# Banded attention and a gated FFN on one core: values matmuls joined to later scores, and other buffers for sums of weights

## The chip, the cores and the metric

One core of a Trainium2 chip runs the whole kernel. The metric is the device time of one execution in microseconds, the median of several runs; the parts of a profile come from one further execution. TensorE, VectorE (DVE), ScalarE (ACT), GpSimd (POOL) and SP's DMA queue each work through a list of their own in order, and wait for one another through semaphores.

## The reference

Eight batches of 576 positions with eight heads of 64 channels go through attention in a band: a query sees itself and the 63 positions before it. The result, as 4608 tokens of 512 channels, goes through a feed-forward network of 2048 hidden units with a gate in place of an activation. All is float32.

```python
scores = (q @ k.T) / sqrt(64)                    # per batch and head
mask = (rel >= 0) & (rel < 64)                   # rel: query position - key position
attn = softmax(where(mask, scores, -1e9))
x = (attn @ v)  as 4608 x 512
h = x @ w_in                                     # 512 x 2048
g = where(h >= 1, h, where(h <= -1, 0, (h + 1) ** 2 / 4))
out = g @ w_out                                  # 2048 x 512
```

## The kernel before, in words

**Tiles and steps.** The tokens are cut into nine tiles of 512. Attention makes a tile in four *steps* of 128 tokens (two blocks of 64 queries, all eight heads). A step has, on TensorE, its **scores** (`att_scores`, L408, small matmuls into two banks `ps_a`) and its **values** (`att_values`, L483, small matmuls from the transposed probabilities `ptd` and the loaded `vt`). Between them lie a mask (L425), a maximum (L429), exponentials on ScalarE (L436), a normalization (L448) and twelve transposes on VectorE (L454). Behind the values, `x_take` copies the bank out to a buffer `u` (L264 on ScalarE, L266 on VectorE), and after two of a tile's steps `add_build` forms the operands of the FFN from it: four differences (L537), then high and low parts (L264/L266 and L549), on ScalarE, VectorE or GpSimd.

**The FFN in three-part products.** Every float32 operand is split into a high and a low part, and a product is the sum of three matmuls. Tiles 0 and 1 multiply x by the weights as they are (`ffn_in`, L877). Tiles 2 to 8 take a pair of hidden chunks at a time, in eight pairs (`ffn_products`, L828): seven products in place of eight, from sums of weights and of x, put together by additions on VectorE (`h_add`, L844). 12 + 12 products come first, then 6 + 12, all into the two banks `ps_h`. The gate follows (ScalarE L889 and L894, VectorE L901, casts L906, low parts on GpSimd L911), and then the output products (L928) into four banks `acc`; gh and gl in the rows below are the gate's high and low part.

**Sums of weights.** They are made once, during tile 1, for the eight pairs (`add_sums`: L736, L745, a cast on ScalarE, L755), and written to DRAM (`kept`). From tile 2 on, each pair's seven operands are loaded from there into *rings* (`add_ring`, `ring_load`) shortly before their use.

**Buffers.** The first layer's weights take 16 places in SBUF, which come free after tile 1 (and after the sums that read them). The tables `X_PIECES`, `R_PIECES`, `H_SLOT` and `TMP_SLOT` say who gets which: operands of x for even and for odd tiles, rings, the hidden values h, and the scratch in which sums are made. In the kernel before, the scratch of pairs 2 to 7 is place 3 and, for the second half of pairs 3 to 7, place 0, which is also that of h: so the first products of tile 2 wait for the sums of the last pair to be kept.

**Order.** A planner (`Plan`) lays all work out before the kernel is built. Each piece of work has a key (about when it is due), costs on the engines that may do it, what it waits for, and slots that it takes from pools and gives back (`ps_a`, `ps_h`, `acc`, `u`, ...). It fills each engine's list with what can start first, lower keys ahead. A whole tile is 21.3 units of keys long. `S_LATE`, `S_LATER` and `S_PACE` set the keys of sums, `A_EARLY` how early the steps of tiles 3 to 8 are due.

**Joined steps.** In `add_step`, a step that is `joined` hands its values on: they are done in one piece with the scores of the next step in the list, by one entry of the planner that also takes a `ps_h` bank for them. Before, steps of tile 2 but its last are joined. All others do their values alone, into a bank of `ps_a`, once the transposes are there. The steps of a tile come in the order 0, 2, 1, 3.

Of the kernel before, what the change touches and what calls it, by code (L numbers as in the profile page):

```python
# [10 lines left out]
F32 = mybir.dt.float32  # L11
# [9 lines left out]
P = 128  # L21
# [18 lines left out]
SOON = 8  # L40
# [46 lines left out]
S_LATE = 3  # L87
S_LATER = 3
S_PACE = 2
X_KEY = 1.3  # L90
# [4 lines left out]
EARLY_2 = 1.5  # L95
X_PIECES = (4, 5, 2), (14, 15)
R_PIECES = (6, 8), (10, 12)
H_SLOT = "w0_0", "w1_0"
TMP_SLOT = "w3_0"
R_LEAD = 6  # L100
R_LOAD = 2800, 2100
A_EARLY = 5

# [89 lines left out]
def banded_attention_then_ffn(ctx: ExitStack, tc: tile.TileContext, q, k, v, w, masks, out, dims):  # L193
# [316 lines left out]
    def x_tiles(t):  # L510
        if t in xops:
            return
        shape = [P, 2, 2, 2, 2 * SB]
        a, b = (xpool.tile(shape, F32R, name="xs", tag=f"{n}{t % 2}") for n in ("xh", "xl"))
        rest = [piece(f).rearrange("p (a c n) -> p a c n", a=2, c=2) for f in X_PIECES[t % 2]]
        if t % 2:
            rest.append(wpool.tile(shape[:1] + shape[2:], F32R, name="xs", tag=TMP_SLOT))
        xops[t] = a, b, rest, [rest[0], a[:, 1], b[:, 0], a[:, 0], rest[1], b[:, 1], rest[2]]
# [66 lines left out]
    def add_step(t, i):  # L585
# [3 lines left out]
        masked = s < PE_MASKS  # L589
        joined = SOON <= s and t <= PLAIN and i < TILES[t] // SB - 1  # L590
        pt, pv = ("ps_h", "acc") if s < LENT else ("ps_a", "ps_a")
# [135 lines left out]
    def sum_whole(n, c, i, eng):  # L727
        if i:
            pass
        elif n < 2:  # L730
            half_of[n, c] = [xpool.tile([P, 8, P], F32, name="half", tag=("xh0", "xl0")[c])]
        else:
            half_of[n, c] = [wpool.tile([P, 8, P], F32, name="half", tag=H_SLOT[0] if n > 2 and c else TMP_SLOT)]
        t = half_of[n, c][0]
        w_ = by_chunk(n)[i]
        engine[eng].tensor_tensor(  # L736
            out=t[:, 2 * i:2 * i + 2], in0=w_[:, 0, c].bitcast(F32), in1=w_[:, 1, c].bitcast(F32), op=ALU.add
        )
# [26 lines left out]
    def add_sums(n):  # L765
        key = step(1) + S_PACE * n + (S_LATE if n < 2 else S_LATER)
        ready = [w_ready[2 * n, 0], w_ready[2 * n + 1, 0]]
        xp = add(key, dict(SP=2000), lambda e: sum_pass(n), ready + [x_in[0]], lag=O_LAG_DMA)
        reads, keeps = [xp], [xp]
        for c in range(2):  # L770
            after = ready + ([x_in[0]] if n < 2 else [l1[1, 3], *sums_read[1]]) + sum_last
            if n == 2 and c:
                after.append(keeps[-1])
            elif n == 3 and not c:
                after.append(sums_kept[2][-1])
            elif n > 2 and c:
                after += [l1[1, 0], *sums_read[0]]
            k = key + c * S_PACE / 2
# [16 lines left out]
    def ring_load(t, n, i):  # L795
        rings[t, n, i] = r = []
        for part in range(2):
            m = 4 - i
            r.append(piece(R_PIECES[i][n % 2] + part)[:, :2 * m * P].rearrange("p (c o n) -> p c o n", c=2, o=m))
            nc.sync.dma_start(out=r[part].bitcast(F32), in_=kept[n][:, part, :, R_OPS[i]])  # L800
# [3 lines left out]
    def add_ring(t, n, i, key):  # L804
        after = [*sums_kept[n], *ring_last[i]]
        if t == PLAIN and n < 2:
            m = R_PIECES[i][n % 2] // 2
            after += [l1[1, 2 * m], l1[1, 2 * m + 1], *sums_read[m]]
        x = add(
# [36 lines left out]
    def add_products(t, n, key, after):  # L846
        ra, rb = (add_ring(t, n, i, key) for i in range(2))
        needs = [ra, *after]
        if t == PLAIN and n < 2:
            needs += [l1[1, 0], l1[1, 1], *sums_read[0], *sums_kept[NF // 2 - 1]]  # L850
        cost, take = dict(DVE=75 + 256 * 1.04), dict(ACT=80 + 256 * .83, DVE=75 + 256 * 1.05)
# [222 lines left out]
    for t in range(len(TILES)):  # L1074
# [4 lines left out]
        if t + 1 == PLAIN:  # L1079
            for n in range(NF // 2):  # L1080
                add_sums(n)
            x_after[t + 1] = [l1[1, f] for f in (2, 4, 5)] + sums_read[1] + sums_read[2] + sums_kept[0] + sums_kept[1]
            x_after[t + 2] = [l1[1, NF - 1], *sums_read[7], *sums_kept[7]]
# [58 lines left out]
```

## Time and profile before

| | |
|---|---|
| runs | 891.44, 891.52, 892.87 us; median 891.52 |
| profiled execution | 890.89 us, span 889.1 us |
| granted TensorE clock | 0.994 |
| TensorE busy | 869.5 us (98%) |
| VectorE, ScalarE, GpSimd busy | 650.4, 508.0, 268.8 us |
| stages of the span | up to some 120 us the first steps and tile 0; then tile 1 with the sums; tile 2 from about 240; from 330 on a tile takes some 94 us; the last tile from 796 has no attention beside it |

How to read the rows: a group's row gives line, engine, operation, output and inputs, shapes and count, then busy time and the mean of one in ns, then the idle time of the engine ahead of it. A row of the timeline gives start, length, engine, line, operation and count, in brackets the idle time ahead and what ended it. Matmuls overlap, so a row's length goes past the start of the next; starts are what counts. One matmul in the program of scores or values is two in the trace (32 become 64, 16 become 32). Windows give the busy time of each engine in a stretch. A wait names who waited, for whom, total us, times, longest.

### The profile page before, as it was taken

What the parts mean: (1) busy time and instruction counts of PE and PEld (TensorE: products, weight loads), DVE (VectorE), ACT (ScalarE), POOL (GpSimd) and SP (SyncE); (2) the same over time, 40 slices, a digit from 0 to 9 for tenths busy, and PEclk for the clock granted to TensorE, in tenths of its full rate; (3) what the DMA queues carried; (4) which work ended last, traced back from release to release, by engine and by line L of the source; (5) the groups of instructions that cost most, each with busy time, mean ns of one, the idle gap of its engine ahead of it and who ended that gap; (6) DMA issues with size and microseconds to landing.
All of it is one profiled execution on the core that took longest, in us unless ns stands there. A gap on an engine that the chain in (4) does not pass through costs nothing.

```text
span 889.1 us, 20426 instructions
## 1 busy us (share of the span) xinstructions
PE 869.5 (98%) x7839; PEld 758.8 (85%) x7839; DVE 650.4 (73%) x1384; ACT 508.0 (57%) x1292; POOL 268.8 (30%) x274
## 2 busy tenths in 40 slices
PE   7899999999999999999999999999999999999998
PEld 5778887877789888888888888888988898899997
DVE  6899997889986867686778687786867676833331
ACT  6999965555654556555554556554654465344443
POOL 1000025565542314232333324231423241322222
PEclk8999999999999999999999999999999999999999
DMA  9992159546676667666666667666865674466531
GB/s 328 409 373 73 38 178 333 177 166 229 233 256 217 219 208 250 205 216 218 219 230 197 218 207 250 201 199 205 280 217 192 216 237 146 156 189 221 169 116 49
DMA packets 107651, 187.61 MB, mean 211 GB/s; under 512 B 8097, under 2 KB 49313, under 8 KB 107553
## 3 DMA queue, kind: packets, MB, share of 16 engines
q1 hardware_dynamic: 107264, 185.38, 62.1%
q8 instruction: 62, 1.02, 0.4%
q10 hardware_dynamic: 288, 0.92, 0.3%
q14 instruction: 37, 0.29, 0.1%
HBM read 162.15 MB, written 24.12 MB: 209 GB/s over the span
## 4 chain that ended last, share of the span: by engine, by line
PE 76%; DVE 15%; ACT 4%; DMA 2%; issue 2%; POOL 1%; SPq 0%; ACTq 0%; DVEq 0%; POOLq 0%
PE acc L928 36%; PE ps_h L828 28%; DVE ptd L454 5%; PE ps_h L877 4%; PE ps_a L483 3%; PE ps_a L408 3%; DVE a L901 2%; ACT sm L436 2%; DVE sm L448 1%; DVE h L844 1%; ACT a L889 1%; DMA vt<-in_v 1%; DMA raw<-in_w 1%; ACT a L894 1%; DVE sm L425 1%
## 5 line engine op out<-in xcount | busy, mean ns | idle before, releaser
L928 PE MATMUL acc<-wts,gh 128*128 128x512 f32 x1154 | 362.1, 395 | 0.5 <-DVE o L266 0.5
L911 POOL TENSOR_TENSOR gl<-a,gh 128x512 fp32r<-128x512 f32 (+1 forms) x130 | 168.5, 1297 | 422.4 <-ACT gh L906 372.9
L928 PEld LDWEIGHTS acc<-wts,gh 128*128 128x128 f32 x1154 | 207.2, 188 | 42.0 <-DVE o L266 0.9
L928 PE MATMUL acc<-wts,gl 128*128 128x512 f32 x577 | 225.4, 391 | 0.3 <-POOL gl L911 0.3
L844 DVE TENSOR_TENSOR h<-h,ps_h 128x256 f32<-128x256 f32 x280 | 117.5, 420 | 126.9 <-PE ps_h L828 112.4
L828 PE MATMUL ps_h<-xs,wts 128*128 128x256 f32 x1488 | 195.9, 282 | 0.1
L828 PEld LDWEIGHTS ps_h<-xs,wts 128*128 128x128 f32 x1488 | 184.8, 189 | 1.7 <-DVE h L844 0.6
L906 ACT CAST gh<-a 128x512 fp32r<-128x512 f32 (+1 forms) x149 | 89.8, 603 | 123.2 <-PE acc L928 102.5
L454 DVE STREAM_TRANSPOSE ptd<-sm 32x256 f32<-32x256 f32 x336 | 146.5, 436 | 6.3
L928 PEld LDWEIGHTS acc<-wts,gl 128*128 128x128 f32 x577 | 108.3, 188 | 24.5 <-POOL gl L911 0.7
L828 PEld LDWEIGHTS ps_h<-wts 128*128 128x128 f32 x864 | 119.6, 189 | 8.7 <-DVE h L844 0.2
L828 PE MATMUL ps_h<-wts 128*128 128x256 f32 x864 | 125.9, 282 | 0.0
L889 ACT ACTIVATE a<-h 128x512 f32<-128x512 f32 x112 | 69.9, 624 | 75.9 <-DVE h L844 73.0
L901 DVE SCALAR_TENSOR_TENSOR a<-a,h 128x512 f32<-128x512 f32 x112 | 85.1, 760 | 30.8 <-ACT a L894 20.4
L436 ACT ACTIVATE sm<-sm,nm 128x96 f32<-128x96 f32 (+1 forms) x256 | 93.1, 366 | 15.5 <-DVE nm L429 15.4
L877 PE MATMUL ps_h<-xh,wts 128*128 128x512 f32 (+1 forms) x296 | 89.6, 372 | 3.8 <-DVE a L901 2.3
L894 ACT ACTIVATE a<-a 128x512 f32<-128x512 f32 (+1 forms) x139 | 86.0, 619 | 4.3
L877 PEld LDWEIGHTS ps_h<-xh,wts 128*128 128x128 f32 x296 | 54.2, 191 | 14.8 <-DVE a L901 3.2
L264 ACT COPY h<-ps_h 128x256 f32<-128x256 f32 x76 | 28.3, 373 | 47.3 <-PE ps_h L828 46.6
L877 PE MATMUL ps_h<-xl,wts 128*128 128x512 f32 (+1 forms) x148 | 54.5, 368 | 0.5 <-DVE xl L496 0.5
L736 POOL TENSOR_TENSOR half<-wts 128x256 f32<-128x256 f32 x17 | 13.3, 799 | 127.0 <-PE ps_h L877 124.5
L436 ACT ACTIVATION_READ_ACCUMULATOR sm<-sm,nm 128x1 f32 x256 | 48.1, 188 | 0.0
(95 smaller groups left out, 801.5 us busy)
## 6 DMA issues: line engine op xcount, KB each, us to landing
wts<-kept SPq DMA_DIRECT2D x112, 512.0 KB, 4.6
wts<-kept SPq DMA_DIRECT2D x112, 384.0 KB, 3.8
vt<-in_v SPq DMA_DIRECT2D x72, 256.0 KB, 4.7
kt<-in_k SPq DMA_DIRECT2D x35, 384.0 KB, 5.5
raw<-in_w SPq DMA_DIRECT2D x12, 1023.8 KB, 10.3
qt<-in_q SPq DMA_DIRECT2D x36, 256.0 KB, 4.8
out<-o SPq DMA_DIRECT2D x33, 256.0 KB, 4.2
kept<-wts SPq DMA_DIRECT2D x24, 256.0 KB, 3.7
```

The source lines that it names most:

```text
L264: nc.scalar.copy(dst, src)
L436: nc.scalar.activation(sm[:, p, :], (ps if masked else sm)[:, p, :], AF.Exp, bias=nm[:, p:p + 1], scale=scale if masked else 1.0, accum_ou ...
L454: nc.vector.transpose(dst[:, :, r], src[:, :, c * SQ:(c + 1) * SQ])
L828: nc.tensor.matmul(ps[:, c * 2 * SB:(c + 1) * 2 * SB], lhsT=r[part][:, cp, o], rhs=xo[k][:, xp, cp], start=i < 2 and c == 0 and j == 0 and ...
L844: nc.vector.tensor_tensor(out=h[:, to:to + 256], in0=h[:, of:of + 256], in1=ps[:, at:at + 256], op=ALU.add)
L877: nc.tensor.matmul(ps, lhsT=wts[f, 0][:, part, c * P:(c + 1) * P], rhs=x[:, c, r], start=(c == 0 and j == 0), stop=(c == NP - 1 and j == 2),)
L889: nc.scalar.activation(gs[t, f, r.start][0], phs[t, f, r.start], AF.Relu, bias=0.5, scale=0.5)
L894: nc.scalar.activation(a, a, AF.Square)
L901: nc.vector.scalar_tensor_tensor(out=a, in0=a, scalar=1.0, in1=ps, op0=ALU.min, op1=ALU.max)
L906: nc.scalar.copy(g[1], g[0])
L911: engine[eng].tensor_tensor(out=g[2], in0=g[0], in1=g[1].bitcast(F32), op=ALU.subtract)
L928: nc.tensor.matmul(acc[t, i][:, n], lhsT=g[:, sub], rhs=wts[f, 1][:, part, n], start=(q == 0 and j == 0), stop=(q == NF - 1 and j == 2 and ...
```

## The change

Three things change. First, `joined` now holds for all four steps of tiles 3 to 7 and for the first three of tile 8 (tile 2 as before); the values of a tile's last step go with the first scores of the next tile. The steps of tiles 3 to 8 are due one key unit earlier (`A_EARLY` 6). Second, the places in SBUF are dealt out anew: the scratch for sums is place 3 for the first half and place 2 for the second, apart from h, and both serve the x of odd tiles later; tile 2's first products wait for fewer sums. Third, the sums of the last two pairs are due 6 key units later (`S_LAST`).

```diff
+S_LAST = 6
...
-X_PIECES = (4, 5, 2), (14, 15)
-R_PIECES = (6, 8), (10, 12)
+X_PIECES = (4, 5, 6), (15,)
+R_PIECES = ((8, 9), (10, 11)), ((12, 13), (7, 14))
 H_SLOT = "w0_0", "w1_0"
-TMP_SLOT = "w3_0"
+TMP_SLOT = "w3_0", "w2_0"
...
-A_EARLY = 5
+A_EARLY = 6
...
-            rest.append(wpool.tile(shape[:1] + shape[2:], F32R, name="xs", tag=TMP_SLOT))
+            rest += [wpool.tile(shape[:1] + shape[2:], F32R, name="xs", tag=tag) for tag in TMP_SLOT]
...
-        joined = SOON <= s and t <= PLAIN and i < TILES[t] // SB - 1
+        joined = SOON <= s and (i < TILES[t] // SB - 1 or PLAIN < t < len(TILES) - 1)
...
-            half_of[n, c] = [wpool.tile([P, 8, P], F32, name="half", tag=H_SLOT[0] if n > 2 and c else TMP_SLOT)]
+            half_of[n, c] = [wpool.tile([P, 8, P], F32, name="half", tag=TMP_SLOT[c])]
...
-        key = step(1) + S_PACE * n + (S_LATE if n < 2 else S_LATER)
+        key = step(1) + S_PACE * n + (S_LATE if n < 2 else S_LATER) + S_LAST * (n > 5)
...
-            after = ready + ([x_in[0]] if n < 2 else [l1[1, 3], *sums_read[1]]) + sum_last
-            if n == 2 and c:
-                after.append(keeps[-1])
-            elif n == 3 and not c:
-                after.append(sums_kept[2][-1])
-            elif n > 2 and c:
-                after += [l1[1, 0], *sums_read[0]]
+            after = ready + ([x_in[0]] if n < 2 else [l1[1, 2], l1[1, 3], *sums_read[1]]) + sum_last
...
-            m = R_PIECES[i][n % 2] // 2
-            after += [l1[1, 2 * m], l1[1, 2 * m + 1], *sums_read[m]]
+            for f in R_PIECES[i][n % 2]:
+                after += [l1[1, f], *sums_read[f // 2]]
...
-            needs += [l1[1, 0], l1[1, 1], *sums_read[0], *sums_kept[NF // 2 - 1]]
+            needs += [l1[1, 0], l1[1, 1], *sums_read[0]]
...
-            x_after[t + 1] = [l1[1, f] for f in (2, 4, 5)] + sums_read[1] + sums_read[2] + sums_kept[0] + sums_kept[1]
+            x_after[t + 1] = [l1[1, f] for f in X_PIECES[0]] + sums_read[2] + sums_read[3] + sums_kept[0] + sums_kept[1]
```

The order of the engines' lists follows from it. On TensorE at a tile's boundary, before: the values of the second step in tile 4's list alone (L483); the scores of the third (L408) follow some products later.

```order
L928 MATMUL acc<-wts,gh 128x512 x2
L928 MATMUL acc<-wts,gl 128x512
L483 MATMUL ps_a<-ptd,vt 64x64 x16
L928 MATMUL acc<-wts,gh 128x512 x2
L928 MATMUL acc<-wts,gl 128x512
L828 MATMUL ps_h<-wts 128x256 x6
L828 MATMUL ps_h<-xs,wts 128x256 x18
```

After, at the same place:

```order
L923 MATMUL acc<-wts,gh 128x512 x2
L923 MATMUL acc<-wts,gl 128x512
L409 MATMUL ps_a<-kt,qt 32x96 x32
L484 MATMUL ps_h<-ptd,vt 64x64 x16
L923 MATMUL acc<-wts,gh 128x512 x2
L923 MATMUL acc<-wts,gl 128x512
```

The scores have moved up to the values, and the values write a bank of `ps_h` instead of `ps_a`. Of TensorE's whole list, 66 excursions to scores or values (30 of scores alone, 30 of values alone, 6 with both) become 44 (8, 8 and 28).

On VectorE, ahead of that boundary's values, before: all transposes (L454) of the step, the last two additions of a pair (L844), the copy of the values (L266) and the gate (L901).

```order
L454 STREAM_TRANSPOSE ptd<-sm 32x8x32 x12
L844 TENSOR_TENSOR h<-h,ps_h 128x256 x2
L266 COPY u<-ps_a 128x512
L901 SCALAR_TENSOR_TENSOR a<-a,h 128x512
L537 TENSOR_TENSOR u<-u 128x256
```

After:

```order
L455 STREAM_TRANSPOSE ptd<-sm 32x8x32 x11
L839 TENSOR_TENSOR h<-h,ps_h 128x256
L455 STREAM_TRANSPOSE ptd<-sm 32x8x32
L839 TENSOR_TENSOR h<-h,ps_h 128x256
L896 SCALAR_TENSOR_TENSOR a<-a,h 128x512
L267 COPY u<-ps_h 128x512
L896 SCALAR_TENSOR_TENSOR a<-a,h 128x512
```

One transpose now stands between the two additions, and the copy of the values behind a gate.

On VectorE near the end of tile 1, between the gates of hidden chunks 12 and 13, before (the last nine of 23 rows between, and the second gate): low parts of x (L549, also into the weights' places), sums of weights (L736, L745, L755) and a step's inverse (L443, L444).

```order
L549 TENSOR_TENSOR xs<-u,xs 128x2x2x128
L736 TENSOR_TENSOR half<-wts 128x256
L549 TENSOR_TENSOR wts<-u,wts 128x2x128
L755 TENSOR_TENSOR half<-half,o 128x512
L549 TENSOR_TENSOR wts<-u,wts 128x2x128
L736 TENSOR_TENSOR half<-wts 128x256
L549 TENSOR_TENSOR wts<-u,wts 128x2x128
L443 TENSOR_SCALAR den<-den 128x8
L444 RECIPROCAL den<-den 128x8
L901 SCALAR_TENSOR_TENSOR a<-a,ps_h 128x512
```

After, all from the one gate to the other:

```order
L896 SCALAR_TENSOR_TENSOR a<-a,ps_h 128x512
L267 COPY u<-ps_a 128x512
L538 TENSOR_TENSOR u<-u 128x256
L449 TENSOR_TENSOR sm<-sm,den 128x384
L538 TENSOR_TENSOR u<-u 128x256
L455 STREAM_TRANSPOSE ptd<-sm 32x8x32 x11
L896 SCALAR_TENSOR_TENSOR a<-a,ps_h 128x512
```

The sums and the low parts of x stand elsewhere now, and a step's transposes stand there instead.

More of the change, by code (lines that the diff above doesn't have):

```diff
@@ L798, in ring_load @@
             m = 4 - i
-            r.append(piece(R_PIECES[i][n % 2] + part)[:, :2 * m * P].rearrange("p (c o n) -> p c o n", c=2, o=m))
+            r.append(piece(R_PIECES[i][n % 2][part])[:, :2 * m * P].rearrange("p (c o n) -> p c o n", c=2, o=m))
             nc.sync.dma_start(out=r[part].bitcast(F32), in_=kept[n][:, part, :, R_OPS[i]])
```

## The prediction

> **What bounds the kernel now.** The page's first part says which engine fills the span.
>
> ```profile
> PE 869.5 (98%) x7839; PEld 758.8 (85%) x7839; DVE 650.4 (73%) x1384; ACT 508.0 (57%) x1292; POOL 268.8 (30%) x274
> ```
>
> TensorE is busy for 869.5 of 889.1 us. A gain can come from two places only: the 19.6 us in which it is idle, and time that counts as busy but does no needed work. The table of windows, read next, separates the stages.
>
> ```profile
> core 0: us, PE busy (x) PEld busy (x) DVE busy (x) ACT busy (x) POOL busy (x), PEclk, DMA share, GB/s
> ...
> 220.00:240.00 20.00, 17.80 (x224) 13.73 (x223) 19.07 (x46) 11.42 (x39) 11.14 (x14) 1.00 0.62 216
> 240.00:260.00 20.00, 18.87 (x158) 16.48 (x158) 18.73 (x44) 12.42 (x29) 9.55 (x10) 1.00 0.86 285
> ...
> 423.87:517.94 94.07, 93.64 (x914) 83.54 (x913) 70.12 (x151) 50.48 (x138) 29.27 (x25) 1.00 0.67 219
> 517.94:611.97 94.03, 93.61 (x913) 83.52 (x913) 70.12 (x151) 50.59 (x138) 29.26 (x25) 1.00 0.66 219
> ```
>
> A tile of the steady part takes 94.05 us and leaves TensorE idle for 0.42 us. Where tile 1 gives way to tile 2 (220 to 260 us) it is idle for 2.20 + 1.13 = 3.3 us, and there VectorE is busy for 37.8 of 40 us: that stretch is VectorE's. The list of who waited for whom, for TensorE over the whole span and then from 330 us on, names the waits that the change can reach.
>
> ```profile
> PE ps_a L483 <- DVE ptd L454: 3.1, 6, 0.9
> PE ps_h L877 <- DVE a L901: 2.3, 2, 1.4
> ```
> ```profile
> PE ps_a L483 <- DVE ptd L454: 2.1, 5, 0.4
> ```
>
> One wait per tile of 0.42 us is the values matmuls (L483) waiting for the last transposes (L454). The rest of a tile is one unbroken stream, so what is left to find is inside the busy time.
>
> **Part 1: scores and values in one piece.** The timeline of TensorE shows what an excursion from the big matmuls costs. First three rows of undisturbed output products, then values alone:
>
> ```profile
> 424.16 0.39 PE L928 MATMUL acc<-wts,gl 128*128 128x512 f32 x1
> 424.39 0.62 PE L928 MATMUL acc<-wts,gh 128*128 128x512 f32 x2
> 424.84 0.39 PE L928 MATMUL acc<-wts,gl 128*128 128x512 f32 x1
> ...
> 431.74 0.40 PE L928 MATMUL acc<-wts,gl 128*128 128x512 f32 x1
> 432.07 1.15 PE L483 MATMUL ps_a<-ptd,vt 128*64 128x64 f32 x32
> 433.15 0.73 PE L928 MATMUL acc<-wts,gh 128*128 128x512 f32 x2
> 433.72 0.39 PE L928 MATMUL acc<-wts,gl 128*128 128x512 f32 x1
> ```
>
> From one gl row to the next it takes 0.68 us undisturbed and 433.72 - 431.74 = 1.98 with the values between: they cost 1.30 us. Their 32 matmuls themselves fill 433.15 - 432.07 = 1.08 of it. About 0.10 is lost going in (432.07 instead of 431.97), and 0.11 coming back (gh to gl 0.57 instead of 0.45). Scores alone:
>
> ```profile
> 462.29 0.88 PE L828 MATMUL ps_h<-xs,wts 128*128 128x256 f32 x6
> 463.00 0.87 PE L828 MATMUL ps_h<-wts 128*128 128x256 f32 x6
> 463.80 1.00 PE L408 MATMUL ps_a<-kt,qt 64*32 64x96 f32 x64
> 464.73 0.73 PE L928 MATMUL acc<-wts,gh 128*128 128x512 f32 x2
> 465.29 0.39 PE L928 MATMUL acc<-wts,gl 128*128 128x512 f32 x1
> ```
>
> Six products take 0.71, and gh to gl 0.45, so 1.16 us without the scores; it took 465.29 - 463.00 = 2.29: scores cost 1.13. Apart, a step costs 1.30 + 1.13 = 2.43. The kernel before already joins three steps of tile 2:
>
> ```profile
> 151.66 0.40 PE L877 MATMUL ps_h<-xl,wts 128*128 128x512 f32 x1
> 151.90 0.40 PE L877 MATMUL ps_h<-xh,wts 128*128 128x512 f32 x1
> 152.23 1.00 PE L408 MATMUL ps_a<-kt,qt 64*32 64x96 f32 x64
> 153.15 1.15 PE L483 MATMUL ps_h<-ptd,vt 128*64 128x64 f32 x32
> 154.23 0.73 PE L928 MATMUL acc<-wts,gh 128*128 128x512 f32 x2
> 154.80 0.39 PE L928 MATMUL acc<-wts,gl 128*128 128x512 f32 x1
> ```
>
> Here 154.80 - 151.66 = 3.14, against 0.24 + 0.23 + 0.45 = 0.92 without the piece: 2.22. One way in and one way back fall away, and **0.21 us per step** is saved. By the instruction order, 30 scores alone, 30 values alone and 6 pieces become 8, 8 and 28: 22 excursions fewer: 22 x 0.21 = 4.6 us. I book **4.4**, at 0.20, as the readings have two decimals. All of it is on TensorE, which sets the end, so it counts in full. Nothing covers it and it cannot be less than zero; its upper bound is the 0.21.
>
> **Part 2: the wait of the values on the transposes.** The third values of each tile start with four matmuls and then stop; rows of TensorE, VectorE and GpSimd:
>
> ```profile
> 480.98 0.34 PE L483 MATMUL ps_a<-ptd,vt 128*64 128x64 f32 x4
> 481.75 1.03 PE L483 MATMUL ps_a<-ptd,vt 128*64 128x64 f32 x28 [0.43 <-DVE ptd L454]
> 482.71 0.73 PE L928 MATMUL acc<-wts,gh 128*128 128x512 f32 x2
> ```
> ```profile
> 479.55 1.69 DVE L901 SCALAR_TENSOR_TENSOR a<-a,h 128x512 f32<-128x512 f32 x1
> 481.25 0.44 DVE L454 STREAM_TRANSPOSE ptd<-sm 32x256 f32<-32x256 f32 x1
> ```
> ```profile
> 479.40 1.29 POOL L911 TENSOR_TENSOR gl<-a,gh 128x512 fp32r<-128x512 f32 x1 [4.28 <-ACT gh L906]
> ```
>
> The values take 482.71 - 480.98 = 1.73 instead of 1.08, so 0.65 us is lost (the list shows about 0.42, since the four early matmuls count as busy). A gate ran for 1.69 us, of which GpSimd's operation covers the first 1.14 (to 480.69), and the last transpose stood behind it. Five tiles: 5 x 0.65 = 3.25.
>
> Where values go with the scores of the next step, they come later. The scores of this step ended at 464.73 (the rows above), so its values had 480.98 - 464.73 = 16.25 us, and needed 0.7 more, 17.0. Twelve output products take 4 x 0.68 = 2.72, and 18 or 24 products 2.13 or 2.84 (0.71 per six). Three of four pieces per tile now have, by the new order, 1.08 + 4 x 2.72 + 2 x 2.84 + 2 x 2.13 + 1.02 = 22.9 us; where only one pair of products lies between (the tile boundary, in the first order rows above) it is 1.08 + 2.72 + 2.84 + 5.44 + 2.13 + 1.36 + 1.02 = 16.6.
>
> ```profile
> L454 DVE STREAM_TRANSPOSE ptd<-sm 32x256 f32<-32x256 f32 x336 | 146.5, 436 | 6.3
> ```
>
> At the boundary VectorE has 11 of the 12 transposes in one go, 11 x 0.44 = 4.8 us, ahead of the addition that waits for the last products, and one behind it. That one ends some 0.42 + 0.44 us after those products, when 1.36 + 1.02 are still to go before the values. So I expect no wait in any tile and book **3.2**. Bounds: 0 (the wait turns up elsewhere) and 3.25.
>
> [...] The order hands 22 of the small sums for x (L537) from VectorE to GpSimd. I still take the 0.65 as removed, since one collision costs 1.0 (1.69 instead of 0.69) and the new places have 22.9 - 17.0 = 5.9 us to spare, or 1.5 at the boundary (2.38 less 0.86).
>
> **Part 3: from tile 1 to tile 2.** TensorE's three longest stops there, and the gate that the first waits for:
>
> ```profile
> 223.34 0.50 PE L877 MATMUL ps_h<-xh,wts 128*128 128x512 f32 x1 [1.42 <-DVE a L901]
> ...
> 234.36 0.98 PE L408 MATMUL ps_a<-kt,qt 64*32 64x96 f32 x62 [0.37 <-ACT u L264]
> ...
> 248.95 1.03 PE L483 MATMUL ps_a<-ptd,vt 128*64 128x64 f32 x28 [0.95 <-DVE ptd L454]
> ```
> ```profile
> 222.65 0.63 DVE L901 SCALAR_TENSOR_TENSOR a<-a,ps_h 128x512 f32<-128x512 f32 x1
> ```
>
> 1.42 + 0.37 + 0.95 = 2.7 us, all of it late work of VectorE or of what hangs on it. The gate at 222.65 has 23 rows between itself and the gate before; in the new order five rows stand between the same two. The scores at 234.36 and the values at 248.95 become parts of joined pieces, further from what they need. New lateness I find in two places. Between the scores of step (2,3) and its values the new order has 1.08 + 2.8 (twelve input products at 0.235) + 1.13 + 2.72 + 5.6 + 2.72 + 0.1 = 16.2 us, against the 16.0 (17.0 less a collision) to 17.0 that the steady step needed: up to 0.8 late, 0.5 taken. And the first additions of tile 2 stand behind five transposes, 5 x 0.44 = 2.2 us, where products six at a time cover 1.36 and less: 0.6 taken. So 2.7 - 1.1 = **1.6**. The sums of the last pairs hardly move: all 40 that VectorE does still come before its first addition of tile 2. Bounds: 2 us lost (another gate as late as the 1.42) and 3.3 gained (every idle us of the two windows).
>
> **What costs nothing.** On SP's queue the second loads of the rings for the first two pairs now wait for later sums, with loads of q, k and v queued behind them.
>
> ```profile
> wts<-kept SPq DMA_DIRECT2D x112, 512.0 KB, 4.6
> ```
>
> Counting the same durations along the order, the first is issued some 20 us before its use and the second, which stands behind a load that waits for the first products of tile 2, some 9 us: a landing of 4.6 is covered twice over. If that cover fails, the lateness is paid once. The counts of matmuls, additions and DMAs are the same; VectorE gains eleven squares and loses the 22 sums, and its 70 of 94 us per tile leave room.
>
> **The sum.** The profiled execution took 890.89 us: the span of 889.1 and 1.8 around it. 890.9 - 4.4 - 3.2 - 1.6 = 881.7. The median of the runs, 891.52, is 0.6 above this execution; I put half of that on top and forecast **882.0**.
>
> **The rivals.**
> First, *the waits only move*: joint values stop for late transposes at other places, and tile 2 starts as badly as before. For it: VectorE's 37.8 of 40 us, and collisions that I cannot place. Against it: 5.9 us to spare in three of four pieces. Then 890.9 - 4.4 = 886.5. Chance 0.27.
>
> Second, *every stop goes*: 890.9 - 4.4 - 3.2 - 3.3 = 880.0, without my 1.1 us of new lateness. Chance 0.15.
>
> Third, *slower, by the bank*: the values now take one of the two ps_h banks that the products alternate in, and the next product can't have it until the values are copied out.
>
> ```profile
> L264 ACT COPY u<-ps_a 128x512 f32<-128x512 f32 x19 | 11.1, 586 | 37.2 <-PE ps_a L483 37.2
> ```
>
> A copy takes 0.59 us. If each of 22 pieces held TensorE up for one copy, that is 13 us, and 890.9 - 9.2 + 13 = 894.7. It decides from 9.2 / 22 = 0.42 us per piece on. The place is the tile boundary, where 1.36 us of output products cover the copy, which VectorE has queued behind a gate. Against it: 2.72 us of output products follow in the other three, and the piece at 153.15 went into ps_h with no stop behind it. [...] No row of this trace shows such a stop. Chance 0.04.
>
> Fourth, *joining saves nothing*, because in the piece the values wait for what they waited for alone: terms 2 and 3 alone, 890.9 - 4.8 = 886.1. The row at 153.15 follows the scores at once, against it. Chance 0.04.
>
> **How the numbers follow.** The forecast has 0.50. The range reaches down to the second rival less a us for the reading of its terms, 879.0, and up to the first at the median's level, 886.5 + 0.6 = 887.1. About 0.2% (1.8 us) is what a measurement of this kernel can tell from no change; all cases but the third lie beyond it on the fast side. Leaving 0.03 for sums of half measures: faster 0.93, same 0.03, slower 0.04.
>
> **What would show it.** Right: tiles 3 to 6 alike at 94.05 - 4 x 0.20 - 0.65 = 92.6 us; a joined piece at 2.2 us; no wait of L483 for L454 after 330 us; fewer than 2 us of TensorE idle between 220 and 260. Wrong: stops of the products behind a copy u out of ps_h, waits of L483 inside the piece, or a first ring load that lands late.

## The result and the profile after

The changed kernel takes 900.21 us (median of 5 runs, 899.54 to 902.13) against 891.52 us before: a ratio of 1.0099, with a 95% interval of 1.0084 to 1.0114. It is slower; the forecast was 882.0 us, with a range up to 887.1. The profiled execution has a span of 898.1 us, 9.0 above the 889.1 of before.

The page's first part, as in the prediction: TensorE does 1.3 us less than before, VectorE 4.4 us more.

```profile
PE 868.2 (97%) x7839; PEld 757.1 (84%) x7839; DVE 654.8 (73%) x1384; ACT 495.4 (55%) x1278; POOL 281.2 (31%) x288
```

To see where the 9.0 us lie, count ScalarE's casts of gates (gh, L901; L906 before) from the end, 16 to a tile. The first cast of tile 2 is at 252.3 us (before 250.0), of tile 3 at 348.2 (340.8), of tile 7 at 726.9 (717.0), of tile 8 at 816.8 (808.3). So 2.3 us are lost up to tile 2, 5.1 in tile 2, 2.5 in tiles 3 to 6 together, 0.5 in tile 8, and 1.4 come back in tile 7. Two stages have to be explained: the steady tiles, which were to fall to 92.6 us each, and tiles 1 and 2.

**A steady tile.** Rows of the table of windows, a tile each (columns as in the prediction), and the list of TensorE's waits from 330 us on:

```profile
430.85:525.43 94.58, 93.31 (x913) 83.13 (x913) 71.21 (x152) 48.29 (x136) 30.37 (x27) 1.00 0.67 218
525.43:620.78 95.35, 93.33 (x914) 83.12 (x913) 71.21 (x152) 48.00 (x134) 30.34 (x27) 1.00 0.68 216
```
```profile
PE ps_h L823 <- DVE h L839: 5.7, 6, 1.2
```

The steady tiles take 94.2 to 95.4 us where they took 94.05. The wait of the values (L484) for the transposes (L455) is gone, as forecast. But products (L823) now wait for additions into h (L839): 1.2 us once a tile, at the boundary of tiles (the second tile above has another stop of 0.85). TensorE's timeline at the tile boundary shows that wait, and behind it a joined piece:

```profile
513.40 0.39 PE L923 MATMUL acc<-wts,gl 128*128 128x512 f32 x1
514.96 0.96 PE L823 MATMUL ps_h<-wts 128*128 128x256 f32 x6 [1.17 <-DVE h L839]
515.94 0.98 PE L823 MATMUL ps_h<-xs,wts 128*128 128x256 f32 x6
516.76 0.87 PE L823 MATMUL ps_h<-wts 128*128 128x256 f32 x6
517.56 1.00 PE L409 MATMUL ps_a<-kt,qt 64*32 64x96 f32 x64
518.49 1.15 PE L484 MATMUL ps_h<-ptd,vt 128*64 128x64 f32 x32
...
520.14 0.39 PE L923 MATMUL acc<-wts,gl 128*128 128x512 f32 x1
```

The piece costs what was forecast: from the last six products to the gl row it is 520.14 - 516.76 = 3.38 us, less 0.71 and 0.45 for what stands there anyway, 2.22. The stop costs more than its label. A gl matmul is followed after 0.23, so products would begin at 513.63; they begin at 514.96, 1.33 late. The next twelve take 516.76 - 514.96 = 1.80 where twelve took 1.42, so 0.38 more: 1.7 us a tile. Part of the 0.38 is a second wait of the same kind, too short for the list: the second six start at 515.94, and the last of the three additions below ends at 514.48 + 1.40 = 515.88. VectorE and GpSimd ahead of it:

```profile
504.69 1.52 DVE L550 TENSOR_TENSOR xs<-u,xs 128x256 fp32r<-128x256 f32 x1
506.14 0.55 DVE L449 TENSOR_TENSOR sm<-sm,den 128x384 f32<-128x384 f32 x1
506.61 0.41 DVE L550 TENSOR_TENSOR xs<-u,xs 128x256 fp32r<-128x256 f32 x1
...
508.95 0.69 DVE L896 SCALAR_TENSOR_TENSOR a<-a,h 128x512 f32<-128x512 f32 x1
509.67 3.58 DVE L455 STREAM_TRANSPOSE ptd<-sm 32x256 f32<-32x256 f32 x8
513.28 0.69 DVE L896 SCALAR_TENSOR_TENSOR a<-a,h 128x512 f32<-128x512 f32 x1
514.01 0.44 DVE L455 STREAM_TRANSPOSE ptd<-sm 32x256 f32<-32x256 f32 x1
514.48 1.40 DVE L839 TENSOR_TENSOR h<-h,ps_h 128x256 f32<-128x256 f32 x3
```
```profile
504.38 1.55 POOL L906 TENSOR_TENSOR gl<-a,gh 128x512 fp32r<-128x512 f32 x1 [0.47 <-ACT gh L901]
```

The additions at 514.48 stand behind nine transposes and two gates. In the same stretch VectorE also builds the x of a coming tile (L550) and normalises (L449). One of its subtractions took 1.52 us instead of the 0.41 of its twin at 506.61, beside GpSimd's gl.

**Tile 1.** The table of windows around TensorE's longest stop, then the links of the chain that led to it: first the chain of waits itself, then VectorE, then TensorE.

```profile
200.00:220.00 20.00, 16.66 (x121) 12.57 (x121) 15.31 (x30) 10.86 (x42) 11.21 (x16) 0.83 0.71 256
```
```profile
197.74 6.50 DMA kept<-half
...
204.37 1.45 POOL half L737 x2
...
208.60 0.63 ACT o L265
209.25 1.23 DVE half L756
```
```profile
209.25 1.23 DVE L756 TENSOR_TENSOR half<-half,o 128x512 fp32r<-128x512 f32 x1 [1.42 <-ACT o L265]
210.40 0.42 DVE L455 STREAM_TRANSPOSE ptd<-sm 32x256 f32<-32x256 f32 x1
210.76 0.64 DVE L896 SCALAR_TENSOR_TENSOR a<-a,ps_h 128x512 f32<-128x512 f32 x1
```
```profile
211.45 0.80 PE L872 MATMUL ps_h<-xh,wts 128*128 128x512 f32 x1 [3.35 <-DVE a L896]
```

VectorE is busy for only 15.3 of 20 us here: it isn't short of time, it stands still. A half of a sum lands 6.5 us after its issue; only then can GpSimd (L737) write the next half into that place; ScalarE's cast waits for GpSimd; VectorE's last subtraction of the sum (L756) waits for the cast; and in VectorE's row the gate that TensorE needs stands behind it. TensorE's granted clock then, by the microsecond:

```profile
210.00:211.00 1.00, 0.00 (x0) 0.77 0.70 270
211.00:212.00 1.00, 0.55 (x1) 0.50 0.68 256
...
216.00:217.00 1.00, 1.00 (x4) 0.50 0.01 2
217.00:218.00 1.00, 1.00 (x5) 0.82 0.00 0
```

Behind the stop the granted clock stays at 0.50 up to 217 us. Twelve products from 211.45 end at 216.74 (5.3 us; 2.8 at 0.235 each), so the 3.35 us cost nearly 6.

**Tile 2.** The chain of waits at the change of tiles goes through the stores of outputs, and TensorE has a stop there for a copy into `o` that the kernel before doesn't have; the chain, then TensorE's row:

```profile
247.09 0.60 ACT o L265
...
247.70 6.85 DMA out<-o
...
255.19 5.54 DMA out<-o
```
```profile
261.47 0.73 PE L923 MATMUL acc<-wts,gh 128*128 128x512 f32 x2 [1.49 <-ACT o L265]
```

An output may only be copied from its bank once the store of an earlier one has freed the tile `o`. The sums use the same two `o` tiles, and the last two pairs' stores (kept<-o) now lie among the outputs'.

### The profile page after: what moved, and what is told of

Same layout as the page of the kernel before. It is cut to its first block, busy times and chain, and to the rows that moved or that the text cites. A ratio compares the mean times of both kernels' runs of the same rounds, so it can differ in the third digit from the quotient of the medians.

```text
span 898.1 us, 20400 instructions
## 1 busy us (share of the span) xinstructions
PE 868.2 (97%) x7839; PEld 757.1 (84%) x7839; DVE 654.8 (73%) x1384; ACT 495.4 (55%) x1278; POOL 281.2 (31%) x288
## 4 chain that ended last, share of the span: by engine, by line
PE 75%; DVE 13%; DMA 5%; ACT 4%; issue 2%; POOL 0%; SPq 0%; ACTq 0%; DVEq 0%; POOLq 0%
PE acc L923 35%; PE ps_h L823 26%; PE ps_h L872 8%; DVE ptd L455 3%; PE ps_a L409 3%; PE ps_h L484 2%; DVE a L896 2%; DMA out<-o 2%; ACT sm L437 2%; DVE h L839 1%; DVE nm L430 1%; DVE sm L449 1%; DMA kt<-in_k 1%; DMA raw<-in_w 1%; DMA kept<-half 1%
## 5 line engine op out<-in xcount | busy, mean ns | idle before, releaser
L906 POOL TENSOR_TENSOR gl<-a,gh 128x512 fp32r<-128x512 f32 (+1 forms) x130 | 169.6, 1306 | 414.5 <-ACT gh L901 359.0
L823 PE MATMUL ps_h<-xs,wts 128*128 128x256 f32 x1632 | 214.0, 282 | 3.4 <-DVE h L839 3.4
L823 PEld LDWEIGHTS ps_h<-xs,wts 128*128 128x128 f32 x1632 | 203.7, 189 | 8.8 <-DVE h L839 6.8
L839 DVE TENSOR_TENSOR h<-h,ps_h 128x256 f32<-128x256 f32 x280 | 117.2, 419 | 120.4 <-PE ps_h L823 104.4
L901 ACT CAST gh<-a 128x512 fp32r<-128x512 f32 (+1 forms) x149 | 89.9, 604 | 156.0 <-PE acc L923 116.9
L455 DVE STREAM_TRANSPOSE ptd<-sm 32x256 f32<-32x256 f32 x336 | 146.3, 436 | 6.2
L884 ACT ACTIVATE a<-h 128x512 f32<-128x512 f32 x112 | 70.1, 626 | 80.0 <-DVE h L839 79.0
L896 DVE SCALAR_TENSOR_TENSOR a<-a,h 128x512 f32<-128x512 f32 x112 | 77.9, 696 | 45.9 <-ACT a L889 44.3
L823 PEld LDWEIGHTS ps_h<-wts 128*128 128x128 f32 x720 | 99.3, 189 | 11.9 <-DVE h L839 5.3
L823 PE MATMUL ps_h<-wts 128*128 128x256 f32 x720 | 105.3, 282 | 3.6 <-DVE h L839 3.5
L437 ACT ACTIVATE sm<-sm,nm 128x96 f32<-128x96 f32 (+1 forms) x256 | 93.5, 368 | 26.7 <-DVE nm L430 26.7
L872 PE MATMUL ps_h<-xh,wts 128*128 128x512 f32 (+1 forms) x296 | 91.6, 378 | 7.4 <-DVE a L896 5.7
L889 ACT ACTIVATE a<-a 128x512 f32<-128x512 f32 (+1 forms) x128 | 79.2, 619 | 3.9
L737 POOL TENSOR_TENSOR half<-wts 128x256 f32<-128x256 f32 x18 | 13.7, 779 | 133.2 <-PE ps_h L872 124.8
```

What stands on the lines that cost most here:

```text
L437: nc.scalar.activation(sm[:, p, :], (ps if masked else sm)[:, p, :], AF.Exp, bias=nm[:, p:p + 1], scale=scale if masked else 1.0, accum_ou ...
L455: nc.vector.transpose(dst[:, :, r], src[:, :, c * SQ:(c + 1) * SQ])
L823: nc.tensor.matmul(ps[:, c * 2 * SB:(c + 1) * 2 * SB], lhsT=r[part][:, cp, o], rhs=xo[k][:, xp, cp], start=i < 2 and c == 0 and j == 0 and ...
L839: nc.vector.tensor_tensor(out=h[:, to:to + 256], in0=h[:, of:of + 256], in1=ps[:, at:at + 256], op=ALU.add)
L872: nc.tensor.matmul(ps, lhsT=wts[f, 0][:, part, c * P:(c + 1) * P], rhs=x[:, c, r], start=(c == 0 and j == 0), stop=(c == NP - 1 and j == 2),)
L884: nc.scalar.activation(gs[t, f, r.start][0], phs[t, f, r.start], AF.Relu, bias=0.5, scale=0.5)
```

## The experiments

All times stand beside runs of the kernel before on the same chip, so the ratios are what compares. "Tiles 1 and 2" is, in each profiled execution, the time from the 128th to the 96th cast of a gate counted from the end; a steady tile is the time between the same scores of two tiles that follow each other (for d2 between the same casts, as its scores change their place from tile to tile).

| kernel | median us | ratio to before (95%) | tiles 1 and 2 | steady tile |
|---|---|---|---|---|
| before | 891.5 | 1 | 195.4 | 94.07 |
| after | 900.2 | 1.0099 (1.0084 to 1.0114) | 202.0 | 94.2 to 95.4 |
| e1 joined alone | 898.0 | 1.0065 (1.0046 to 1.0083) | 200.0 | 94.70 |
| e2 places alone | 893.3 | 1.0019 (1.0006 to 1.0032) | 196.7 | 94.0, one 95.6 |
| e3 after, A_EARLY 5 | 898.1 | 1.0069 (1.0049 to 1.0089) | 198.5 | 94.69 |
| e4 after, S_LAST 0 | 902.2 | 1.0111 (1.0092 to 1.0129) | 203.9 | 94.4 |
| h1 after, short transposes | 886.0 | 0.9932 (0.9917 to 0.9947) | 195.7 | 92.5 to 93.5 |
| h2 before, short transposes | 885.4 | 0.9938 (0.9920 to 0.9956) | 191.8 | 93.42 |
| h3 joined alone, short transposes | 886.8 | 0.9949 (0.9935 to 0.9963) | 194.9 | 93.33 |
| s1 after, subtraction on GpSimd | 898.6 | 1.0074 (1.0061 to 1.0088) | 201.3 | 94.2 to 95.0 |
| j1 takes joined | 888.1 | 0.9958 (0.9945 to 0.9970) | 197.6 | 92.88 |
| j2 builds joined | 895.1 | 1.0032 (1.0019 to 1.0045) | 199.8 | 93.64 |
| a6 before, A_EARLY 6 | 907.7 | 1.0175 (1.0161 to 1.0190) | 206.5 | 95.86 |
| d1 build first | 897.4 | 1.0064 (1.0052 to 1.0076) | 199.0 | 94.97 |
| d2 build late | 894.1 | 1.0020 (1.0010 to 1.0029) | 199.2 | 93.0 and 94.15 |
| d3 build later | 892.0 | 1.0000 (0.9989 to 1.0010) | 198.2 | 93.32 |
| p1 after, takes joined, A_EARLY 5 | 890.1 | 0.9984 (0.9975 to 0.9992) | 197.7 | 92.94 |
| j4 takes joined, A_EARLY 4 | 896.9 | 1.0055 (1.0042 to 1.0069) | 203.6 | 93.6 to 94.7 |
| w1 takes joined, subtraction on GpSimd | 891.3 | 0.9994 (0.9985 to 1.0003) | 200.0 | 92.9 to 93.6 |

### The parts apart: e1 to e4

My first theory laid the loss on tile 2 and the places; its rival on the joined steps.

e1 takes only the line on `joined` into the kernel before:

```diff
-        joined = SOON <= s and t <= PLAIN and i < TILES[t] // SB - 1
+        joined = SOON <= s and (i < TILES[t] // SB - 1 or PLAIN < t < len(TILES) - 1)
```

> The kernel before with the joined steps alone: places, sums, S_LAST and A_EARLY stay as before. Theory T1 (the loss lies in tile 2: the new places and the later sums make a stop of 3.35 us there, and the halved clock behind it; joining itself saves 0.3 to 0.8 us a tile and gives back 1.2 to 2 us a tile in waits of products for h_add): tile 2 ends as before at 330 us, steady tiles between 93.2 and 94.6 us, total 888 to 893, most likely 890.5. Theory T2 (joining moves the order of VectorE's work in tile 2 as well and is the cause of the stop): 897 to 901.

e2 undoes that line, and `A_EARLY`, in the changed kernel.

> The changed kernel with the joined steps undone and A_EARLY back at 5: the new places and S_LAST = 6 remain. T1: the stop near 208 us and the low clock behind it remain, tile 2 ends 5 to 7 us later than before, steady tiles 94.05 us as before, total 896 to 898.5. T2: no stop of 3 us, total 891 to 893.

Joined alone takes 898.0 us, the places with the late sums alone 893.3. My theory fell: some 6 of the 8.7 us belong to the joined steps, under 2 to the places. e2's profiled execution is 2.3 us longer than that of before, and 1.5 of it is one steady tile of 95.6 us, in which values wait 1.4 us for transposes. In e1 tiles 1 and 2 are 4.7 us longer than before (the stop of 1.42 us before is 2.39 here, and the granted clock behind it 0.50, see the end), and every steady tile is longer too. The window of one tile of e1 (columns as before, line numbers of the kernel before):

```profile
447.91:542.61 94.70, 93.73 (x913) 83.22 (x912) 73.65 (x154) 47.66 (x131) 30.80 (x27) 1.00 0.66 219
```

94.70 us: the steady tiles are lengthened by the joining itself, by 0.65 us. Their stops are not quite those of the changed kernel; TensorE's waits in e1 from 330 us on:

```profile
PE acc L928 <- POOL gl L911: 2.5, 4, 0.6
PE ps_h L828 <- DVE h L844: 1.7, 5, 0.4
```

Once a tile an output product waits for GpSimd's gl, whose gate stands behind transposes in VectorE's row, and once products wait for the additions. e3 and e4 change one number of the changed kernel each: `A_EARLY = 5`, and `S_LAST = 0`.

> The changed kernel with A_EARLY = 5 in place of 6. T1: the stop in tile 2 stays (tile 2 ends near 336 us). If the scores placed one unit earlier put the transposes ahead of h_add in VectorE's row, the waits of products for h_add go, steady tiles are near 93.3 us and the total is 895; if the joined pieces make these waits by themselves, steady tiles stay at 94.5 us or more and the total is 899 to 902.

> The changed kernel with S_LAST = 0: the last two pairs of sums in their old place in time. T1 with the places as the cause (the stop near 208 us is in the sums of a pair ahead of the last two): the stop stays, 899 to 902. Rival: the later last pairs moved the whole row of the sums and made the stop; then it goes, and tile 2 ends 3 to 5 us earlier: 893 to 896.

e3: 898.1 us, 2 less than the changed kernel (the two intervals just overlap). The steady tiles stay at 94.69, with the stops of e1 (0.62 and 0.35 us) in place of the one of 1.2: the earlier scores don't cause the loss, they only change who is waited for. Tiles 1 and 2 are 3.5 us shorter. e4: the stop near 208 us stays (3.97 us), so the late pairs don't make it. But among the seven kernels with the new places e4 alone has no stop of output products for a copy into `o` between 245 and 262 us. With `S_LAST = 6` the others have 0.85 to 2.63 us of it (1.49 in the changed kernel). So the late sums do cost there, and without them more is lost elsewhere.

### VectorE or the bank: h1 to h3

Each transposes only 2 of 8 heads per instruction (0.24 in place of 0.44 us) and leaves the other six out, so that their values come from old numbers; order and TensorE's work stay:

```diff
-        nc.vector.transpose(dst[:, :, r], src[:, :, c * SQ:(c + 1) * SQ])
+        nc.vector.transpose(dst[:, :2, r], src[:, :2, c * SQ:(c + 1) * SQ])
```

> The changed kernel with every transpose L455 reading and writing 2 of its 8 heads (32x64 in place of 32x256; the other heads keep old numbers): the order on every engine is the same, TensorE's work is the same, VectorE is freed of about 4 us a step. Theory V (the stops of the joined steady tiles come from VectorE's row, in which h_add and the gate stand behind transposes that run late): no stop of products for h_add after 330 us, steady tiles 92.7 to 93.0 us, 888 to 893 us in all. Theory B (the values in a bank of ps_h make the products wait for that bank): the stops and 94.5 us a tile stay, 898 to 901 us.

> The kernel before with the same short transposes. V: the wait of the values for the transposes goes, steady tiles 93.3 us in place of 94.05, 885 to 888 us. This is the second term of the prediction (3.2 us) by itself.

> The joined steps alone on the kernel before, with the same short transposes. V: no steady stop, tiles 92.7 to 92.9 us, 0.5 to 0.8 us a tile below the kernel before with short transposes, so 881 to 885 us: joining then gains what the first term of the prediction says, once VectorE is out of the way. B: tiles stay at 94.2 us or more, 893 to 898 us.

One tile each of h2, h3 and h1:

```profile
435.88:529.30 93.42, 93.42 (x913) 83.44 (x912) 59.34 (x151) 50.43 (x137) 29.31 (x25) 1.00 0.66 219
```
```profile
438.77:532.10 93.33, 93.18 (x913) 83.16 (x912) 64.51 (x154) 47.38 (x131) 30.55 (x27) 1.00 0.66 221
```
```profile
484.42:577.62 93.20, 92.79 (x914) 83.14 (x913) 61.68 (x152) 47.68 (x133) 30.41 (x27) 1.00 0.66 221
```

With some 10 us a tile taken off VectorE alone, the three kernels lie within 1.4 us of each other, and the changed one gains some 14 us by it, more than expected, though three waits of products for additions (0.4 to 0.8 us) stay in its steady tiles. So it is VectorE's lateness, not the bank, that costs. h2 is the second term of the prediction measured by itself: 94.07 - 93.42 = 0.65 us a tile. The surprise is h3: joining gains 0.09 us a tile where 0.5 to 0.8 was expected, though the list shows no wait of TensorE in its steady tiles. Its timeline has waits too short for the list; here a gl matmul on TensorE, and the gl that it needs on GpSimd:

```profile
598.65 0.61 PE L928 MATMUL acc<-wts,gh 128*128 128x512 f32 x2
599.34 0.50 PE L928 MATMUL acc<-wts,gl 128*128 128x512 f32 x1
599.67 0.62 PE L928 MATMUL acc<-wts,gh 128*128 128x512 f32 x2
```
```profile
597.99 1.29 POOL L911 TENSOR_TENSOR gl<-a,gh 128x512 fp32r<-128x512 f32 x1 [4.16 <-ACT gh L906]
```

gh to gl takes 0.69 and not 0.45, gl to gh 0.33 and not 0.23: 0.34 us lost, at the very end of GpSimd's operation (599.28). This tile's twelve matmuls from 598.65 take 3.09 in place of 2.75, and three from 621.44 take 0.93 in place of 0.69: most of what is missing.

### Which joined steps: j1 and j2

The values of the steps 0 and 1 of a tile are only taken out of the bank into u. Those of 2 and 3 complete a pair and set off the build of x: differences, casts and subtractions (L537, L266, L549) on VectorE, ScalarE and GpSimd. From tile 3 on, j1 joins the first kind alone and j2 the second, in the kernel before:

```diff
-        joined = SOON <= s and t <= PLAIN and i < TILES[t] // SB - 1
+        joined = SOON <= s and (t <= PLAIN and i < TILES[t] // SB - 1 or PLAIN < t < len(TILES) - 1 and i < 2)
```

> The kernel before with values joined, from tile 3 on, only for the steps 0 and 1 of a tile, whose values are only taken into u (x_take) and start no build of the products' operands. Theory V with the build as the culprit (the stops come when the build of x, some 5 us of VectorE and GpSimd, falls into the same stretch as the softmax of the step joined with it): two joins a tile save 0.4 us, no new stop; steady tiles 93.0 to 93.7 us, 887 to 890.5 us. Theory V without it (any joined step makes VectorE late): tiles of 94.3 us or more, 893 to 896 us.

> The kernel before with values joined, from tile 3 on, only for the steps 2 and 3 of a tile, whose values complete a build. V with the build as the culprit: the stops of the changed kernel are all here, steady tiles 94.3 to 95.0 us, 893.5 to 898 us. V without it: half of the loss of the joined steps alone, 94.4 us, 893 to 895 us, the same as its counterpart with takes joined.

One tile of j1:

```profile
440.53:533.41 92.88, 92.88 (x913) 83.28 (x912) 71.99 (x157) 49.09 (x132) 27.88 (x24) 1.00 0.67 222
```

j1 has no stop left in a steady tile: 94.07 - 0.65 (the wait) - 0.54 for two joins. At 888.1 us it beats both kernels, and no other one tried is as fast with all of the work done. j2's total is in the expected range, but not for the expected reason: its steady tile is 93.64 us, shorter than before, and what it loses it loses in tiles 1 and 2 (199.8 against 195.4). So joined builds alone don't bring the stops of the steady tiles, but for one of 0.2 us a tile. All four together do: 94.70.

### Order, or a burst: d1 to d3

All four joined, as in e1. d1 gives the taking and the build of joined values an earlier due time, d2 and d3 a later one:

```diff
-            split(xs, key, "ps_h")
+            split(xs, key - B_STEP * (t > PLAIN), "ps_h")   # d1; d2: key + 1.5 * (t > PLAIN); d3: key + 3 * (t > PLAIN)
```

> The joined steps alone, with the due time of the taking and the build of joined values (from tile 3 on) set back by one step (16/3 units), so that they stand ahead of the softmax and of h_add in VectorE's row, as they do where values are done alone. If the joined tiles lose because the join hands the build a later due time: tiles of 92.9 to 93.6 us, 888 to 893 us. If they lose because the build and the softmax come into one stretch whatever their order: 94.5 us or more, 896 to 900 us.

> The joined steps alone, with that due time set 1.5 units (some 6 us) later, so that the softmax and the gates go ahead of the build. If the burst of build and softmax is what makes VectorE late: the two are parted, tiles of 92.7 to 93.6 us, 888 to 893 us. If any joined build costs: 94.5 us or more, 896 to 900 us.

> The joined steps alone with the due time of joined takes and builds 3 units later in place of 1.5 (which gave 93.0 and 94.15 us in turn, 894.1 us in all). If parting build and softmax is what counts: every steady tile 92.6 to 93.2 us, 889 to 893 us. If the tiles that stay at 94.15 us do so for another reason: 893.5 to 896 us.

One tile of d1 and one of d3:

```profile
443.38:538.35 94.97, 93.74 (x914) 83.30 (x913) 68.66 (x146) 48.93 (x136) 33.87 (x30) 1.00 0.66 217
```
```profile
442.20:535.52 93.32, 93.16 (x914) 83.38 (x913) 67.78 (x141) 51.42 (x139) 35.24 (x32) 1.00 0.67 221
```

With the build first the tile is longer still than in e1, though VectorE is busy for less (68.7 us) than in the kernel before (70.1). With the build 3 units later every tile takes 93.32 us, 1.4 less than in e1, with the same joined pieces and the same work. d2 cures every second tile. So the stops come neither from the joined piece nor from too little time on VectorE, but from where the build stands and who does it. That the later due time parts the build from the softmax is not shown: in d3, too, a subtraction of the build (L549) stands directly ahead of the transposes. VectorE's rows at the second build of these tiles, first of e1, then of d3:

```profile
508.97 1.22 DVE L549 TENSOR_TENSOR xs<-u,xs 128x512 fp32r<-128x512 f32 x1
510.12 0.43 DVE L454 STREAM_TRANSPOSE ptd<-sm 32x256 f32<-32x256 f32 x1
```
```profile
499.36 0.68 DVE L549 TENSOR_TENSOR xs<-u,xs 128x512 fp32r<-128x512 f32 x1
499.96 1.77 DVE L454 STREAM_TRANSPOSE ptd<-sm 32x256 f32<-32x256 f32 x4
```

The joined piece starts at 496.26 in e1 and at 489.11 in d3, so the transposes begin 13.9 us behind it in e1 and 10.9 in d3. What changed with it is the sharing: of taking and building x VectorE does 11.2 us a tile in e1 and 2.8 in d3, ScalarE and GpSimd the rest. Less on VectorE isn't enough by itself, as d1 has 3.8 us there and stops, and j1 9.0 and doesn't. Of the two things that the due time changes, place and engine, no run changes one alone. d3's 93.32 just misses the 93.2 that I had expected as the upper end; a stop of 0.17 us stays. Its total of 892.0 is that of the kernel before, since tiles 1 and 2 keep a loss of 3 us.

### A_EARLY, the sums' row, and combinations: a6, j4, s1, w1, p1

a6 sets `A_EARLY = 6` in the kernel before; j4 sets it to 4 in j1.

> The kernel before with A_EARLY = 6 alone (scores from tile 3 on one unit of the plan, some 6 us, earlier). The changed kernel lost 2.1 us more than the same kernel with A_EARLY = 5. If the earlier scores cost by themselves: 892.5 to 895 us. If they cost only together with the joined steps: 890.5 to 892 us, with the wait of values for transposes of 0.43 us gone or moved.

> The kernel before with the takes joined and A_EARLY = 4. A_EARLY = 6 alone cost 15.5 us by waits of values for transposes (1.9 us a tile) and stops in tile 2. If a later start of the scores only lengthens the lead of the transposes: 886 to 889 us, steady tiles 92.9 us. If the plan is simply fitted to 5: over 890 us.

Both missed upward, at 907.7 and 896.9 us. In a6 the values wait for the transposes in every tile; the list of waits for one of its tiles:

```profile
PE ps_a L483 <- DVE ptd L454: 1.9, 3, 1.0
```

The plan is fitted to 5. That a unit either way moves VectorE's row against the products is how I read these waits; no run takes that apart.

s1 and w1 put the subtraction that held the gate in tile 1 on GpSimd, s1 in the changed kernel, w1 in j1:

```diff
-        engine[eng].tensor_tensor(out=t[:, 4:].bitcast(F32R), in0=t[:, 4:], in1=h, op=ALU.subtract)
+        engine["Pool" if n > 1 else eng].tensor_tensor(out=t[:, 4:].bitcast(F32R), in0=t[:, 4:], in1=h, op=ALU.subtract)
```

> The changed kernel with the last subtraction of each pair of sums from pair 2 on (L756) always on GpSimd in place of VectorE; the order is the same otherwise. Theory S (the stop of 3.35 us near 208 us comes from VectorE standing at that subtraction for ScalarE's cast, that for GpSimd's sums, and these for the store of an earlier half): the stop is under 1.5 us, the clock stays at 1.00 behind it, tile 2 ends 4 to 6 us earlier, 894 to 896.5 us. Rival: the products wait for the whole chain of sums anyway, the stop stays over 3 us, 899 to 902 us.

> The takes joined alone (888.1 us), with the last subtraction of each pair of sums from pair 2 on (L755) on GpSimd in place of VectorE. Its trace has a stop of 2.47 us at 224 us and the clock low behind it, since VectorE has two such subtractions and the build ahead of a gate. If they make that stop: it is under 1.5 us, the clock stays up, 884.5 to 887 us. If the build alone holds the gate: 887.5 to 889.5 us.

In s1 the stop of 3.35 us becomes 0.38, which shows the last link of the chain above right. But 1.57 and 0.62 us come back some 5 us later, as output products wait for gh and gl, and with 898.6 us s1 misses its range. In w1 the stop near 224 us shrinks from 2.47 to 1.73, and one of 1.50 us appears at 182: at 891.3 us it is slower than j1. (The granted clock behind j1's stop is 1.00, and not low as the expectation has it.) Taking one link out of the sums' chain moves the stop.

> The changed kernel with only the takes joined (steps 0 and 1 of a tile from tile 3 on) and A_EARLY = 5: the new places and S_LAST = 6 stay. From the runs apart: places 1.6 us slower, takes joined 4.1 us faster than before; if the two add, 889 to 890 us, steady tiles 92.9 us. If the places need the joined builds or gain with them: 886 to 888 us.

p1: 890.1 us, just above what the parts add up to; steady tiles 92.94 us. Places and late sums bring nothing to the takes joined.

## Why the prediction was wrong

Of the 18 us between forecast and result, some 8 lie in tiles 3 to 6 (378.6 us by the casts, where four tiles at 92.6 make 370.4) and some 8 in tiles 1 and 2 (6.6 lost where 1.6 were to be gained).

**Term 1, scores and values in one piece (4.4 us): the size was right, the cover was not.** A joined piece costs 2.22 us as forecast, and two joins a tile give 0.54 in j1, a little more than 2 x 0.20. But the term was booked as wholly on TensorE with nothing that could be worse. Joining also changes when VectorE gets its work: with all four joined, h3 shows 0.09 us a tile left of it even with short transposes, and e1 a loss of 0.65.

**Term 2, the wait of the values (3.2 us): it went, and another one took its place.** This is the step that failed. It compared 22.9 and 16.6 us of cover with the 17.0 that the *values* need, and asked of the additions only whether the transposes behind them were late for the values. It counted 11 transposes, 4.8 us, ahead of the addition at the boundary and did not ask who waits for that addition: the next products, within the same pair. They stop there for 1.2 us, 1.7 with what follows, against the 0.65 removed. For tile 2 term 3 did ask just that, of five transposes (2.2 us) ahead of additions that 1.36 us of products cover; for the steady tiles, with more than twice as many, it wasn't asked. Rival 1 (the waits only move) was nearest in kind, but it let them move at their old price.

The prediction booked nothing for VectorE and GpSimd meeting, since one collision, at 1.0 us, had room. One lies in this row, some 9 us ahead of the stop: the subtraction of 1.52 us beside GpSimd's gl, in place of 0.41. Of the changed kernel's 16 subtractions of this shape on VectorE (L550, 128x256) the six beside GpSimd's work take 1.51 or 1.52 us and the ten others 0.41 or 0.42; the 18 of 128x512 take 0.68 or 0.69, beside it or not. The 1.1 us are nearly the length of the stop, and no run parts this collision from the rest of the row.

**Term 3, tiles 1 and 2 (1.6 us, bounds 2 lost to 3.3 gained): both sign and bound were wrong.** Tiles 1 and 2 together took 202.0 us instead of 195.4, 6.6 more. The stops were read off the order row by row, for the rows that I knew from before. The stop of 3.35 us comes from a place that none of them had: VectorE standing at a sum's subtraction for a store. And no term held the granted clock of 0.50 behind the stop, which made the twelve products there take 5.3 us in place of 2.8. I wrote that the last sums hardly move. For VectorE's share that is so (its last sum ends at 240.1 us, the first addition starts at 244.9), but GpSimd's last sum ends at 263.5 us in place of 234.4, and the stores came to lie among those of the outputs (1.5 us).

**Costs nothing.** The ring loads cost nothing that a run shows. But `A_EARLY = 6` had no term at all: it costs 15.5 us in the kernel before, and some 2 us in the changed one. And "its 70 of 94 us leave room" took an average over a tile for room at a place: d1's steady tile is longer than e1's with less work on VectorE. The count was short as well: VectorE loses the 22 small sums, but takes 12 subtractions of the build (L550) from GpSimd, 34 where it did 22.

**The third rival** (slower, by the bank) gave 894.7 us, on the right side, but by another mechanism: no stop behind a copy out of ps_h appears in a steady tile, and short transposes take the loss away with the banks unchanged.

What stays open: why two joined builds without joined takes keep the steady tiles short and four joined steps don't; whether d3 cures its tiles by the place of the build or by the engines that do it; and how the 2 to 5 us that joined kernels lose in tiles 1 and 2 divide between the plan's order and the landings of stores (6.85 and 5.54 us in the changed kernel's chain of tile 2).

## What to carry to other kernels

When a wait goes because something is moved, ask of each in-order engine what now stands ahead of what the bound engine needs next, not only whether the moved thing is in time. Room on average is no room at a place: join or move only what starts no further work on that engine, as the takes did here (888.1 us), and look whether other engines can do the burst that must come, as they did in d3. A stop can cost more than its length: in shorter waits behind it, which a list of waits leaves out (0.38 us behind the 1.33 of the boundary), and in the granted clock (0.50 behind the 3.35 us of tile 1, which cost nearly 6 in all).

## What the runs showed of the hardware

The granted clock behind a stop doesn't follow from the stop's length alone. In e1 it was 0.50 behind a stop of 2.39 us, in e3 1.00 behind one of 2.63; TensorE's rows, and the windows beside them, first of e1, then of e3:

```profile
226.46 0.79 PE L877 MATMUL ps_h<-xh,wts 128*128 128x512 f32 x1 [2.39 <-DVE a L901]
```
```profile
226.00:227.00 1.00, 0.54 (x1) 0.55 0.88 152
227.00:228.00 1.00, 1.00 (x4) 0.50 0.99 341
```
```profile
250.39 0.73 PE L923 MATMUL acc<-wts,gh 128*128 128x512 f32 x2 [2.63 <-ACT o L265]
```
```profile
250.00:252.00 2.00, 1.33 (x5) 1.00 1.02 374
```

In j1 a stop of 2.47 us, ahead of 223.87, left the clock at 1.00 too. In the kernel before, stops of 1.47 and 0.49 us, ahead of 23.99 and 24.86, had 0.50 behind them from 25 to 28 us, and one of 1.42, ahead of 223.34, had 1.00. What else than the length decides, no run shows.
